# Raw scores stored negated, their column maximum added by an accumulating DMA, running maxima kept pairwise in SBUF, and new instruction orders

## The chip, the cores and the metric

The kernel runs on one core of a Trainium2 chip. The metric is the device time of one execution in microseconds (us). Five instruction queues run side by side and meet at semaphores: TensorE (PE in the profile), VectorE (DVE), ScalarE (ACT), GpSimd (POOL) and SyncE (SP), which here only issues DMAs. Each queue runs its instructions strictly in the order in which the program was written. Matrix products land in PSUM, which TensorE, VectorE and ScalarE reach; GpSimd and DMAs work on SBUF and HBM only.

## The reference

```python
def _A_ref(x, wqkv, wo):                      # S = 2048, D = 448, H = 16, Dh = 28
    qkv = (x @ wqkv).reshape(B, S, 3, H, Dh).transpose(2, 0, 3, 1, 4)
    q, k, v = qkv[0], qkv[1], qkv[2]
    scores = einsum("bhqd,bhkd->bhqk", q, k) * (Dh ** -0.5)
    p = softmax(scores, axis=-1)
    o = einsum("bhqk,bhkd->bhqd", p, v)
    return o.transpose(0, 2, 1, 3).reshape(B, S, D) @ wo
def _B_ref(x, W_gate, W_up, W_down):          # F = 1792
    gate = x @ W_gate; up = x @ W_up
    gate = gate * (gate > 0)
    return (gate * up) @ W_down
g = sigmoid((x * gate_w).sum(-1, keepdims=True))
return g * _A_ref(x, wqkv, wo) + (1 - g) * _B_ref(x, W_gate, W_up, W_down)
```

All tensors are float32. The kernel multiplies with rounded float32 operands and splits each operand into a high part and a low part (the rest), so that several products make up one exact one; `TERMS` lists the eleven products for a depth of 448.

## The kernel before, in words

Three stages follow each other. First the projections: `qk` and `vproj` make queries, keys and values from x, and write queries and keys to HBM. Last comes the feed-forward tail: `down`, `wout` and `result`. Between them, from about 137 us to about 1076 us, lies the attention, 32 visits long, and the first 51 of 56 gate-and-up units of the feed-forward part are laid between its instructions as filling.

A visit is one head (28 channels) and one half of the keys (1024 of 2048). It makes 16 score tiles of 128 keys x 1024 (two chunks of 128 x 512, in PSUM); together they cover all 2048 queries, in four blocks of 512. For query blocks 0 to 2 the softmax maximum is known beforehand: `smax` (line 169) computes the scores a second time with queries on partitions, VectorE reduces them (L171), and `smax_end` writes the negated maximum into spare rows of Q, so that the score product already has it subtracted. ScalarE then takes exp straight out of PSUM (L260). For the last query block (j = 3, four of the sixteen tiles, the "late" ones) the maximum is found from the transposed scores themselves: ScalarE copies the raw scores to SBUF (L262); `block_max` (L228) folds the two chunks of each tile into a running maximum `rm` of 128 x 512 on VectorE, reading PSUM; `all_max` (L234) takes the maximum over partitions on GpSimd; `take_max` (L239) subtracts it on VectorE from each of the two groups of 128 x 2048; `take_exp` (L246) takes exp of a group on ScalarE. `rescale` (L585 to L589) brings the first half's result to the second half's maximum. `pv` (L601) multiplies with the values, in two parts P and Q of 32 matmuls each, the whole 64 taking 7.0 us; P reads the first group, Q the second.

The order is written out by hand as a string for each visit: `FIRST` for visit 0, `LONG` for 24 visits, `WIDE` for 4, and `LATE` for the last 3. A letter is one action: `s` a score tile (two matmuls and the ScalarE instruction that empties it), `m` one `smax` step (two matmuls and one VectorE reduction), `x` one of the eleven matmuls of half a gate-and-up unit, `A` `all_max`, `d` `take_max`, `e` `take_exp`, `n` `smax_end`, `c` and `f` the two parts of `rescale`, `w` the splitting of the next gate-and-up weights (`split_f`), `P` and `Q` the two parts of `pv`. In `FIRST`, `l` sends the last projected keys and `u` splits the second half of the first weights and clears a query buffer. The scores run `AHEAD` = 3 tiles ahead of the visit, so three of a visit's four late tiles are computed near the end of the visit before, and the fourth at its own start.

PSUM holds the score and `smax` tiles in three buffers that are used in turn (`ps_w`), whatever reads them. So a tile's matmuls wait until the tile three before has been read. `split_f` takes the high part of the weights on ScalarE (`act_high`, L103) and the low part, in the attention stage, on GpSimd (`pool_low`, L112).

Of the kernel before, what the change touches and what calls it, by code (L numbers as in the profile page):

```python
# [19 lines left out]
P = 128  # L20
S = 2048
D = 448
H = 16
# [5 lines left out]
NB = 4  # L29
TB = 512  # L30
NK = S // P
SCALE = DH ** -0.5
# [34 lines left out]
def gated_mix_kernel(ctx, tc, x, wq, wo, wgu, wd, out):  # L67
    nc = tc.nc
# [137 lines left out]

    stream = [p for v in range(2 * H) for p in visit(v)]
    todo_max, todo_sub, todo_exp, todo_all = [], [], [], []
    RM = {}

    def block_max(v, j, k, p, q):

        n = TQ[v // 2]
        b = j - NB + n
        if (v, b) not in RM:
            if b == 0:
                rm = att.tile([P, max(TQ), TB], F32, name=f"rm_{v}", tag=f"rm{v % 2}", bufs=1)
                for c in range(n):
                    RM[v, c] = rm[:, c]
        r = RM[v, b]  # L220
        if k % (NK // 2):
            parts = [(p[:, c], r) for c in range(2)]
        elif v % 2:
            parts = [(p[:, 0], RM[v - 1, b]), (p[:, 1], r)]
        else:
            parts = [(p[:, 0], q[:, 1])]
        for x, y in parts:
            nc.vector.tensor_tensor(r, x, y, op=OP.max)  # L228
        if k % (NK // 2) == NK // 2 - 2:
            todo_all.append((v, b, [(v, j, i) for i in (k // 4 - 1, k // 4)]))  # L230

    def all_max():
        v, b, quads = todo_all.pop(0)
# [2 lines left out]

    def take_max():
        v, b, q = todo_sub.pop(0)
        nc.vector.tensor_tensor(QUAD[q], QUAD[q], RM[v, b].unsqueeze(1).to_broadcast([P, 4, TB]), op=OP.subtract)  # L239
        todo_exp.append(q)  # L240

    def take_exp():
        q = min(todo_exp, key=lambda q: (q[0], q[2], q[1]))
        todo_exp.remove(q)
        q = QUAD[q].rearrange("p c t -> p (c t)")
        nc.scalar.activation(q, q, AF.Exp, scale=SCALE)  # L246

    def score(late=True):

        v, done, q, half, chunks = stream.pop(0)  # L250
        h = v // 2
        if q not in QUAD:
            QUAD[q] = p_slot(next(slots) % NP, f"P_{v}_{q[1]}_{q[2]}")
        ps = ps_w(f"s_{v}_{chunks[0][0]}_{chunks[0][1]}")
        for c, (k, j) in enumerate(chunks):
            nc.tensor.matmul(ps[:, c], K[h % 3][:, k * P:(k + 1) * P], Q[h][:, j * TB:(j + 1) * TB], start=True, stop=True)  # L256
            AT[v, k, j] = QUAD[q][:, 2 * half + c]
        dst = QUAD[q][:, 2 * half:2 * half + 2]
        if done:
            nc.scalar.activation(dst, ps, AF.Exp, scale=SCALE)  # L260
        else:
            nc.scalar.activation(dst, ps, AF.Copy)  # L262
# [25 lines left out]
    with tc.tile_pool(name="qkv", bufs=1) as pa:  # L288
# [187 lines left out]
        for n, (f, *a) in enumerate(mixed):  # L476
            if n == 0:
                split_w(*w5)
            if n == 6:
                load_k(1)  # L480
                load_q(1)
            if n == 8:
                split_w(*w3)
            if n == 13:

                nc.gpsimd.memset(f32(K[2])[96:128], -1.0)
            if n == len(mixed) - 6:
# [8 lines left out]
            news = [(score, False) for back in EARLY if back == len(mixed) - n]  # L496
# [22 lines left out]
    def split_f(i, high, low, part=(0, 1)):  # L519

        if part[0] == 0:
            WS[i] = fe.tile([P, 2, 7, P], F32R, name=f"wg_{i}", tag="wg", bufs=2)
        w, wr = WS[i], WR[i]
        for s in part:
            high(w[:, s, 0:3], wr[:, s, 0:3])
            low(w[:, s, 3:6], wr[:, s, 0:3], w[:, s, 0:3])
        if part[-1] == 1:
            high(w[:, :, 6], wr[:, :, 3])
            low(w[64:, :, 6], wr[64:, :, 3], w[64:, :, 6])
            del WR[i]  # L530
            ws_d[i] = dram.tile([P, 2, 7, P], F32, name=f"ws_d_{i}")
            nc.sync.dma_start(ws_d[i], f32(w))
# [58 lines left out]
    PO = {}  # L591
# [63 lines left out]
        if h and q == 2:  # L655
            normalise(h - 1)

    split_f(0, act_high, pool_low, (0,))
    fetch_f(1)
    while todo_max:  # L660
        block_max(*todo_max.pop(0))
    for v, (order, nu) in enumerate(ROUNDS):
        todo = list(range(nxt, nxt + nu))
        nxt += nu
        small_things(2 * v)
        passes = [(*divmod(k, 2), n) for k in todo for n in range(NT)]
        units = []
        ns = 0
        for o in order:
            if o == "x" and not passes:  # L670
                continue
            if o == "s":
                ns += 1
                if ns == 8:
                    small_things(2 * v + 1)
                if stream:
                    score()
            elif o == "m":
                if m < len(maxima):
                    smax(m)  # L680
                    m += 1
            elif o == "x":
                i, half, n = passes.pop(0)
                if n == 0:
                    units.append((i, half, ps_x(f"gu_{i}_{half}")))
                gu_mm(units[-1][2], i, half, n)
                if n == NT - 1:
                    i, half, ps = units.pop()
                    spill_h(i, ps) if half else relu(i, ps)
                    if half:  # L690
                        load_f(i + 2)
            elif o == "n":
                if v % 2 and v < 2 * H - 1:
                    smax_end(v // 2 + 1)
            elif o == "w":
                ready = nxt + (ROUNDS[v + 1][1] if v + 1 < len(ROUNDS) else 2)
                ready = min(ready + ready % 2, 2 * NF)
                while parts < ready:
                    split_f(parts // 2, act_high, pool_low, (parts % 2,))
                    parts += 1  # L700
                    if parts % 2 == 0:
                        fetch_f(parts // 2 + 1)
            elif o == "A":
                all_max()
            elif o == "d":
                take_max()
            elif o == "e":
                take_exp()
            elif o in "cf":
                rescale(v, "cf".index(o))  # L710
            elif o == "l":
                sends.pop()()
            elif o == "u":
                split_f(0, act_high, pool_low, (1,))
                QS.append(last_q("Q2"))
                nc.gpsimd.memset(f32(QS[2])[96:128], 0.0)
# [6 lines left out]
        left = [k for k in todo_exp + todo_sub + todo_all if k[0] == v]  # L723
        assert not passes and not left and v not in PO or len(stream) == max(0, 16 * (2 * H - 1 - v) - AHEAD), (v, passes, left, len(stream) + 16 * (v + 1))
    assert not stream and m == len(maxima), (len(stream), m)
    stk.close()

# [181 lines left out]
```

## Time and profile before

| | |
|---|---|
| median of 3 runs | 1284.88 us (1283.1 to 1288.92) |
| the profiled execution | 1281.88 us, its span 1280.1 us |
| busy, TensorE / VectorE / ScalarE / GpSimd | 1241.6 / 962.1 / 776.1 / 191.2 us |
| span from the first P of visit 0 to the first P of visit 28 | 821.88 us |
| mean share of time that the 16 DMA engines are busy, in that stretch | 0.42 |

A busy TensorE is not TensorE at its peak: matmuls overlap each other, and one row's duration (about 398 ns) is longer than the distance from one to the next. The distance is read from the chain of work that ended last, which lists consecutive matmuls without overlap. The idle time in front of an instruction is named with what released it. In the tables by stretch of time the columns are: length, busy time of TensorE, of its weight loads, of VectorE, ScalarE and GpSimd (with their numbers of instructions), the granted TensorE clock as a share of full speed, the busy share of the DMA engines, and GB/s.

### The profile page before, as it was taken

Reading aid. Unit: us, or ns where it says so; the run is one execution under the profiler, and the core shown is the slowest. Engines: PE = TensorE matmul, PEld = TensorE weight load, DVE = VectorE, ACT = ScalarE, POOL = GpSimd, SP = SyncE. Lnnn points to the kernel's source line nnn. Section 1 sums busy time; section 2 is a strip of 40 time slices with the busy share of each in tenths; the row PEclk is TensorE's granted clock in tenths of the full one; section 3 lists DMA queues with packets and bytes.
Section 4 is the critical chain, followed back from the end, with each engine's and each line's share of the span. In section 5 each row is a group of like instructions: output and inputs, shape, how many; then the busy total and the mean of one; then the engine's idle time right before and its main releaser. Section 6 shows DMA issues by size and latency. Waiting matters only on the chain.

```text
span 1280.1 us, 16867 instructions
## 1 busy us (share of the span) xinstructions
PE 1241.6 (97%) x6431; PEld 872.5 (68%) x6431; DVE 962.1 (75%) x1022; ACT 776.1 (61%) x894; POOL 191.2 (15%) x188
## 2 busy tenths in 40 slices
PE   9999699999999999999999999999999999999998
PEld 6888466665656666666666566666666566799998
DVE  6466679898988989998988889898989543563342
ACT  5223377777877677777777677767777784122121
POOL 4222221221221000000000001000000010551020
PEclk9999899999999999999999999999999999999999
DMA  9845275352626543342536243342442325745432
GB/s 323 289 189 222 84 209 117 127 163 72 169 76 201 169 121 84 103 133 64 163 104 186 81 113 103 84 130 93 132 128 76 119 90 195 228 147 159 132 115 80
DMA packets 64269, 178.37 MB, mean 139 GB/s; under 512 B 13730, under 2 KB 20578, under 8 KB 59554
## 3 DMA queue, kind: packets, MB, share of 16 engines
q1 hardware_dynamic: 57452, 151.00, 39.5%
q0 software_dynamic: 6304, 25.82, 5.3%
q8 instruction: 51, 0.84, 0.3%
q10 hardware_dynamic: 432, 0.46, 0.1%
q14 instruction: 30, 0.25, 0.1%
HBM read 118.58 MB, written 58.87 MB: 139 GB/s over the span
## 4 chain that ended last, share of the span: by engine, by line
PE 89%; DVE 4%; ACT 2%; DMA 2%; issue 1%; POOL 1%; SPq 0%; POOLq 0%; ACTq 0%
PE gu L547 19%; PE s L256 19%; PE po L601 18%; PE sm L169 13%; PE acc L808 10%; PE qk L381 5%; DVE rm L228 3%; PE wo L767 3%; PE v L399 3%; ACT P L262 1%; DVE mx L171 1%; DMA wg<-ws_d 1%; DMA or<-o_d 0%; DMA wr<-wq 0%; ACT P L260 0%
## 5 line engine op out<-in xcount | busy, mean ns | idle before, releaser
L171 DVE TENSOR_REDUCE mx<-sm 128x1 f32<-128x1024 f32 x384 | 456.5, 1219 | 60.6 <-PE sm L169 59.5
L547 PE MATMUL gu<-X,wg 128*128 128x512 f32 x1232 | 373.9, 398 | 10.8 <-POOL wg L112 7.2
L260 ACT ACTIVATE P<-s 128x1024 f32<-128x1024 f32 x306 | 306.7, 1025 | 116.8 <-PE s L256 113.1
L256 PE MATMUL s<-Q,K 128*128 128x512 f32 x1024 | 319.5, 403 | 13.6 <-DVE rm L228 11.2
L547 PEld LDWEIGHTS gu<-X,wg 128*128 128x128 f32 x1232 | 231.6, 189 | 69.1 <-POOL wg L112 7.6
L256 PEld LDWEIGHTS s<-Q,K 128*128 128x128 f32 x1024 | 184.7, 189 | 99.3 <-DVE rm L228 10.9
L169 PE MATMUL sm<-K,Q 128*128 128x512 f32 x768 | 243.2, 398 | 7.5 <-DVE mx L171 3.6
L601 PE MATMUL po<-P,V 128*32 128x512 f32 x1640 | 227.3, 594 | 0.0
L228 DVE TENSOR_TENSOR rm<-s,rm 128x512 f32<-128x512 f32 x218 | 150.4, 690 | 74.6 <-ACT P L262 57.3
L169 PEld LDWEIGHTS sm<-K,Q 128*128 128x128 f32 x768 | 137.1, 188 | 52.6 <-ACT P L260 10.1
L234 POOL PARTITION_ALL_REDUCE rm<-rm x32 | 57.2, 1788 | 673.7 <-DVE rm L228 618.8
L601 PEld LDWEIGHTS po<-P,V 128*32 128x32 f32 x1640 | 62.6, 110 | 116.2 <-issue 111.5
L808 PE MATMUL acc<-WD,hh 128*128 128x448 f32 x672 | 138.5, 365 | 0.0
L262 ACT ACTIVATE P<-s 128x1024 f32<-128x1024 f32 x104 | 105.1, 1024 | 46.6 <-PE s L256 45.4
L808 PEld LDWEIGHTS acc<-WD,hh 128*128 128x128 f32 x672 | 126.2, 188 | 10.4
L239 DVE TENSOR_TENSOR P<-P,rm 128x2048 f32<-128x2048 f32 x52 | 117.9, 2272 | 5.8 <-POOL rm L234 5.8
L601 PE MATMUL po<-V 128*32 128x512 f32 x408 | 115.0, 594 | 0.0
L103 ACT ACTIVATE hh<-hr 128x512 fp32r<-128x512 f32 x56 | 35.2, 631 | 117.8 <-PE acc L808 113.8
L246 ACT ACTIVATE P<-P 128x2048 f32<-128x2048 f32 x52 | 99.4, 1914 | 5.3 <-DVE P L239 4.5
L260 ACT ACTIVATE V<-s 128x1024 f32<-128x1024 f32 x78 | 78.9, 1025 | 37.1 <-PE s L256 35.2
L109 DVE TENSOR_TENSOR hh<-hr,hh 128x512 fp32r<-128x512 f32 x56 | 49.4, 883 | 62.2 <-ACT hh L103 62.2
L381 PE MATMUL qk<-X,W 128*128 128x512 f32 x308 | 77.4, 398 | 0.3 <-DVE X L109 0.2
(79 smaller groups left out, 772.4 us busy)
## 6 DMA issues: line engine op xcount, KB each, us to landing
wg<-ws_d SPq DMA_DIRECT2D x42, 896.0 KB
K<-qk_d SPq DMA_DIRECT2D x64, 224.0 KB
Q<-qk_d SPq DMA_DIRECT2D x64, 224.0 KB
h_d<-h SPq DMA_DIRECT2D x56, 256.0 KB
hr<-h_d SPq DMA_DIRECT2D x56, 256.0 KB
ws_d<-wg SPq DMA_DIRECT2D x14, 896.0 KB
qk_d<-st POOLq DMA_DIRECT2D x21, 512.0 KB, 3.2
wgr<-wgu SPq DMA_DIRECT2D x13, 512.0 KB
```

The source lines that it names most:

```text
L169: nc.tensor.matmul(ps[:, c, :], Q[h][:, u * P:(u + 1) * P], K[h % 3][:, k0:k0 + TB], start=True, stop=True)
L171: nc.vector.tensor_reduce(MX[h][:, 2 * u + half:2 * u + half + 1], ps, axis=AX.XY, op=OP.max)
L228: nc.vector.tensor_tensor(r, x, y, op=OP.max)
L239: nc.vector.tensor_tensor(QUAD[q], QUAD[q], RM[v, b].unsqueeze(1).to_broadcast([P, 4, TB]), op=OP.subtract)
L246: nc.scalar.activation(q, q, AF.Exp, scale=SCALE)
L256: nc.tensor.matmul(ps[:, c], K[h % 3][:, k * P:(k + 1) * P], Q[h][:, j * TB:(j + 1) * TB], start=True, stop=True)
L260: nc.scalar.activation(dst, ps, AF.Exp, scale=SCALE)
L262: nc.scalar.activation(dst, ps, AF.Copy)
L381: nc.tensor.matmul(ps, W[:, a, c * P:(c + 1) * P], xf(tb, b), start=(n == 0), stop=(n == NT - 1))
L547: nc.tensor.matmul(ps, WS[i][:, s, a], xf(i // NF, b), start=(n == 0), stop=(n == NT - 1))
L601: nc.tensor.matmul(po[32 * j:32 * j + 32], V[:, h // 4 % 2, k, h % 4], AT.pop((v, k, j)), start=(k == k0), stop=(k == k0 + NK // 2 - 1))
L808: nc.tensor.matmul(ACC[i // NF][t][:, :D], HH[i][:, a, t * P:(t + 1) * P], WD[:, f, b], start=(f == 0 and n == 0), stop=(f == NF - 1 and n ...
```

## The change

The raw scores of the late tiles are copied out of PSUM with the sign turned (`scale=-1.0`), so the running maximum becomes a running minimum. It is no longer read from PSUM: the new `block_min` (letter `b`, three per visit) folds whole 128 x 1024 tiles in SBUF into a pair `r2`, and the third one folds the pair into `rm` (128 x 512), and turns the sign back. For the second half of the keys the last step also takes the maximum with the first half's `rm`. `take_max` becomes a DMA that GpSimd issues; it adds `rm`, repeated four times, to the group of 128 x 2048 in SBUF (1024 KB each, two per visit, 64 in all). The exp after it uses `scale=-SCALE`. All four late tiles of a visit are now computed in the visit before (`AHEAD` = 4). The low parts of the gate-and-up weights are computed on VectorE (`low`) in place of GpSimd (`pool_low`). The four order strings are new; the numbers of `s`, `m` and `x` in `LONG`, `WIDE` and `LATE` are as before.

```diff
-AHEAD = 3
+AHEAD = 4
-FIRST = "AmxmxsmxmxxlxsxumsmmmxxxsxdxxxsxssmxxmxsmmxdexxsxsewsPQ"
-LONG = "ssmnAxxxxsmxsxmxsmxxxmsmxxxsmxxmxsdxsxxxsxsmxxxsmxxmexxsmxxdxxcsxsefwsPQ"
-WIDE = "smnmxxxxxxxsxxmxxxxmsxmxxsmxxsAmxsxmxxsxsmxdxsxxsssxxxmxxxcsxmsxxdxxmxxxxexsxewsPfQ"
-LATE = "snwsxxAxdxxxsxxsxxxsxxdsxxxxcsxxsxxxsxxxsxxxxsxsxxxxsxxxxxexxxsxxessPfQ"
+FIRST = "xxxbsbbmxmlxssmsxxmuAddsxxsmsxxmxsmsxmsxmxbxsmxmxbxxxesxmebPwQ"
+LONG = "nssAddxxxxmxsxmxxsmxsxmxsxsxmxxsxmsxmxxsmxsxmxssxcxsmxexxmxxxssbxxbbexfmPwQ"
+WIDE = "ssAddnscxxxsxxxmxxxsxxmxsxmxsxmxsxxxmsxxmfxsxxsmsxxxxmxxsxmsxmxxxxmbxexsxxsxbemxxbxPwQ"
+LATE = "nsAddsxxcxsxsxsxxxxxsxxsxssxxxxsxxsxxxssxxwxxexsxxxxxxxbxxxxssxbxxbxexxPfQ"
...
+    def block_min():
...
+        v, j, p = todo_max[0]
+        b = j - NB + TQ[v // 2]
+        if (v, b) not in R2:
+            R2[v, b] = att.tile([P, 2, TB], F32, name=f"r2_{v}_{b}", tag="r2", bufs=1)
+            left[v, b] = NK // 4 - 2
+            nc.vector.tensor_tensor(R2[v, b], todo_max.pop(0)[2], todo_max.pop(0)[2], op=OP.min)
+            return
+        nc.vector.tensor_tensor(R2[v, b], R2[v, b], todo_max.pop(0)[2], op=OP.min)
...
+        nc.vector.tensor_tensor(r, r2[:, 0], r2[:, 1], op=OP.min)
+        if v % 2:
+            nc.vector.scalar_tensor_tensor(r, r, -1.0, RM[v - 1, b], op0=OP.mult, op1=OP.max)
         else:
-            parts = [(p[:, 0], q[:, 1])]
-        for x, y in parts:
-            nc.vector.tensor_tensor(r, x, y, op=OP.max)
...
+            nc.vector.tensor_scalar(r, r, -1.0, None, op0=OP.mult)
...
     def take_max():
         v, b, q = todo_sub.pop(0)
-        nc.vector.tensor_tensor(QUAD[q], QUAD[q], RM[v, b].unsqueeze(1).to_broadcast([P, 4, TB]), op=OP.subtract)
+        nc.gpsimd.dma_start(QUAD[q], RM[v, b].unsqueeze(1).to_broadcast([P, 4, TB]), accum_op=OP.add)
...
-        nc.scalar.activation(q, q, AF.Exp, scale=SCALE)
+        nc.scalar.activation(q, q, AF.Exp, scale=-SCALE)
...
-            nc.scalar.activation(dst, ps, AF.Copy)
-            job = (v, chunks[0][1], chunks[0][0], ps if late else dst, dst)
-            if late:
-                block_max(*job)
-            else:
-                todo_max.append(job)
+            nc.scalar.activation(dst, ps, AF.Copy, scale=-1.0)
+            todo_max.append((v, chunks[0][1], dst))
...
-    split_f(0, act_high, pool_low, (0,))
+    split_f(0, act_high, low, (0,))
     fetch_f(1)
-    while todo_max:
-        block_max(*todo_max.pop(0))
...
-                if ns == 8:
+                if ns == 10:
                     small_things(2 * v + 1)
...
-                    split_f(parts // 2, act_high, pool_low, (parts % 2,))
+                    split_f(parts // 2, act_high, low, (parts % 2,))
...
+            elif o == "b":
+                block_min()
...
-                split_f(0, act_high, pool_low, (1,))
+                split_f(0, act_high, low, (1,))
```

More of the change, by code (lines that the diff above doesn't have):

```diff
@@ L39 @@
 EARLY = (5, 4, 4, 3, 2, 2, 1, 1)
-AHEAD = 3
+AHEAD = 4
 NP = 10
-FIRST = "AmxmxsmxmxxlxsxumsmmmxxxsxdxxxsxssmxxmxsmmxdexxsxsewsPQ"
-LONG = "ssmnAxxxxsmxsxmxsmxxxmsmxxxsmxxmxsdxsxxxsxsmxxxsmxxmexxsmxxdxxcsxsefwsPQ"
-WIDE = "smnmxxxxxxxsxxmxxxxmsxmxxsmxxsAmxsxmxxsxsmxdxsxxsssxxxmxxxcsxmsxxdxxmxxxxexsxewsPfQ"
-LATE = "snwsxxAxdxxxsxxsxxxsxxdsxxxxcsxxsxxxsxxxsxxxxsxsxxxxsxxxxxexxxsxxessPfQ"
+FIRST = "xxxbsbbmxmlxssmsxxmuAddsxxsmsxxmxsmxsmxsmxbxsmxmxbxxxesxmebPwQ"
+LONG = "nssAddxxxxmxsxmxxsmxsxmxsxsxmxxsxmsxmxxsmxsxmxssxcxsmxexxmxxxssbxxbbexfmPwQ"
+WIDE = "ssAddnscxxxsxxxmxxxsxxmxsxmxsxmxsxxxmsxxmfxsxxsmsxxxxmxxsxmsxmxxxxmbxexsxxsxbemxxbxPwQ"
+LATE = "nsAddsxxcxsxsxsxxxxxsxxsxssxxxxsxxsxxxssxxwxxexsxxxxxxxbxxxxssxbxxbxexxPfQ"
 ROUNDS = [(FIRST, 2)] + [(WIDE, 4) if k % 7 == 2 else (LONG, 3) for k in range(2 * H - 4)] + [(LATE, 4)] * 3
@@ L208, in gated_mix_kernel @@
     todo_max, todo_sub, todo_exp, todo_all = [], [], [], []
[L209 to L224, printed above, removed]
-        else:
-            parts = [(p[:, 0], q[:, 1])]
-        for x, y in parts:
-            nc.vector.tensor_tensor(r, x, y, op=OP.max)
-        if k % (NK // 2) == NK // 2 - 2:
-            todo_all.append((v, b, [(v, j, i) for i in (k // 4 - 1, k // 4)]))
+    RM, R2, left = {}, {}, {}
+    def block_min():
+        if not todo_max:
+            return
[5 more added lines that the diff above has]
+            nc.vector.tensor_tensor(R2[v, b], todo_max.pop(0)[2], todo_max.pop(0)[2], op=OP.min)
+            return
+        nc.vector.tensor_tensor(R2[v, b], R2[v, b], todo_max.pop(0)[2], op=OP.min)
+        left[v, b] -= 1
+        if left[v, b]:
+            return
+        r, r2 = att.tile([P, TB], F32, name=f"rm_{v}_{b}", tag=f"rm{v % 2}{b}", bufs=1), R2[v, b]
+        RM[v, b] = r
+        nc.vector.tensor_tensor(r, r2[:, 0], r2[:, 1], op=OP.min)
+        if v % 2:
+            nc.vector.scalar_tensor_tensor(r, r, -1.0, RM[v - 1, b], op0=OP.mult, op1=OP.max)
+        else:
+            nc.vector.tensor_scalar(r, r, -1.0, None, op0=OP.mult)
+        q = NK // 8 * (v % 2)
+        todo_all.append((v, b, [(v, j, q), (v, j, q + 1)]))
     def all_max():
@@ L245, in take_exp, with score @@
         q = QUAD[q].rearrange("p c t -> p (c t)")
-        nc.scalar.activation(q, q, AF.Exp, scale=SCALE)
-    def score(late=True):
+        nc.scalar.activation(q, q, AF.Exp, scale=-SCALE)
+    def score():
         v, done, q, half, chunks = stream.pop(0)
@@ L495, in gated_mix_kernel @@
                 m += 1
-            news = [(score, False) for back in EARLY if back == len(mixed) - n]
+            news = [(score,) for back in EARLY if back == len(mixed) - n]
             for k, c in enumerate(news):
@@ L722, in gated_mix_kernel @@
                 pv(v, "PQ".index(o))
-        left = [k for k in todo_exp + todo_sub + todo_all if k[0] == v]
-        assert not passes and not left and v not in PO or len(stream) == max(0, 16 * (2 * H - 1 - v) - AHEAD), (v, passes, left, len(stream) + 16 * (v + 1))
+        rest = [k for k in todo_exp + todo_sub + todo_all if k[0] == v]
+        assert not passes and not rest and v not in PO or len(stream) == max(0, 16 * (2 * H - 1 - v) - AHEAD), (v, passes, rest, len(stream) + 16 * (v + 1))
     assert not stream and m == len(maxima), (len(stream), m)
```

## The prediction

> **What bounds the kernel now.** I read the page first, then the chain of work that ended last, then busy time by stretch.
>
> ```profile
> span 1280.1 us, 16867 instructions
> PE 1241.6 (97%) x6431; PEld 872.5 (68%) x6431; DVE 962.1 (75%) x1022; ACT 776.1 (61%) x894; POOL 191.2 (15%) x188
> PE 89%; DVE 4%; ACT 2%; DMA 2%; issue 1%; POOL 1%; SPq 0%; POOLq 0%; ACTq 0%
> ```
>
> TensorE carries 89% of the chain, so anything taken off VectorE is worth only the time in which TensorE waits for it. The page's run took 1281.88 us, 3.0 us under the median of 1284.88; the sum below is made against 1281.9. One `LONG` visit on the chain (start, length, what), with the bounds of others:
>
> ```profile
> 170.32 7.24 PE po L601 x64
> ...
> 199.47 7.00 PE po L601 x64
> ...
> 495.06 7.00 PE po L601 x64
> 502.06 0.68 PE s L256 x2
> ...
> 502.76 1.03 ACT P L262
> ...
> 503.82 0.70 DVE rm L228
> ...
> 504.54 0.70 DVE rm L228
> ...
> 505.38 0.70 PE s L256 x2
> 506.08 0.47 PE sm L169 x2
> ...
> 509.15 0.70 PE gu L547 x3
> ...
> 524.05 7.00 PE po L601 x64
> ...
> 992.20 7.00 PE po L601 x64
> 1017.17 7.00 PE po L601 x64
> ```
>
> Unhindered matmuls follow each other every 0.70/3 = 0.2325 us, and the 64 of `po` take 7.0. A `LONG` visit has 33 `x`, 16 `s` and 12 `m`, 33 + 32 + 24 = 89 matmuls: 20.7 + 7.0 = 27.7 us at full pace, against 28.99 from 495.06 to 524.05. Nearly all that is missing lies in one place. After `po`, ScalarE copies the late tile, VectorE folds its two chunks out of PSUM, and only then is the buffer free for the tile three later. From 502.06 to 506.08 there are 12 matmuls (four `s`, two `sm`, four `gu`, two `s` again), 2.79 us of work in 4.02: 1.23 lost, of which 0.68 - 0.465 = 0.22 is the switch from `po`, which stays. So 1.0 us per visit waits for the chain ACT L262, DVE L228, DVE L228.
>
> Over the stage: 170.32 to 992.20 is 821.9 us for 24 `LONG` and 4 `WIDE` visits (11 more matmuls, 30.25 at full pace). 24 x 27.69 + 4 x 30.25 = 785.6; so 36.3 us are lost in all, 1.30 per visit, which agrees. From 992.20 to 1017.17, a `LATE` visit, it is 24.97 against 17.67 + 7.0 = 24.67: nothing to win there.
>
> ```profile
> 495.06:524.05 28.99, 28.19 (x157) 18.21 (x161) 26.03 (x28) 21.04 (x22) 1.83 (x2) 1.00 0.46 116
> 137.00:170.00 33.00, 21.27 (x66) 14.46 (x66) 21.96 (x25) 13.16 (x18) 7.35 (x7) 0.79 0.42 111
> 170.32:992.20 821.88, 804.88 (x4347) 519.42 (x4350) 730.36 (x744) 603.51 (x644) 87.77 (x81) 1.00 0.42 122
> ```
>
> The second row is `FIRST`: TensorE idles 11.7 of 33 us, and the clock granted there is 0.79.
>
> **The change part by part.**
>
> ```profile
> L171 DVE TENSOR_REDUCE mx<-sm 128x1 f32<-128x1024 f32 x384 | 456.5, 1219 | 60.6 <-PE sm L169 59.5
> L228 DVE TENSOR_TENSOR rm<-s,rm 128x512 f32<-128x512 f32 x218 | 150.4, 690 | 74.6 <-ACT P L262 57.3
> L239 DVE TENSOR_TENSOR P<-P,rm 128x2048 f32<-128x2048 f32 x52 | 117.9, 2272 | 5.8 <-POOL rm L234 5.8
> L262 ACT ACTIVATE P<-s 128x1024 f32<-128x1024 f32 x104 | 105.1, 1024 | 46.6 <-PE s L256 45.4
> L246 ACT ACTIVATE P<-P 128x2048 f32<-128x2048 f32 x52 | 99.4, 1914 | 5.3 <-DVE P L239 4.5
> L234 POOL PARTITION_ALL_REDUCE rm<-rm x32 | 57.2, 1788 | 673.7 <-DVE rm L228 618.8
> L109 DVE TENSOR_TENSOR W<-wr,W 128x336 fp32r<-128x336 f32 (+6 forms) x20 | 8.2, 435 | 5.9 <-ACT W L103 5.6
> x_d<-X POOLq DMA_DIRECT2D x6, 1024.0 KB, 5.1
> qk_d<-K POOLq DMA_DIRECT2D x6, 512.0 KB, 6.9
> ```
>
> *VectorE.* Removed per visit: 7.5 folds (7 or 8 by turns) x 0.69 = 5.2 and 2 subtractions x 2.27 = 4.5. Added: 3 minima of 128 x 1024 (half a subtraction 1.14, two folds 1.38; I take 1.2, nearer the subtraction, which is in SBUF too) = 3.6; a last fold 0.7; the sign, between nothing and another fold, 0.4. That is 9.7 against 4.7: 26.0 busy in the quoted visit becomes 21.0. The low parts of the weights: 28 of 128 x 384 at some 0.49 (435 ns for 336 columns, scaled) and 14 smaller ones at 0.36, 19 us in all, 2 us in each of the first ten visits; 23 of 28 there is still room, so I cost it at nothing. What would take that cover away is in the next paragraphs: VectorE standing still.
>
> *The PSUM wait.* The fourth late tile moves into the visit before (`AHEAD` = 4), and PSUM is released by the copy alone. After `po` the first two tiles are plain exps, and `LONG` puts four `x` and a `m` before the third. The 1.0 us goes. What is late next there is the ScalarE copy, 1.0 us after its matmuls, with 1.6 us to go before the buffer is wanted again.
>
> *ScalarE.* The negated copy is the same instruction with another constant: 1.02 us, no cost. But its order matters. Counting 0.2325 per matmul in the new `LONG`, scores stand at 14.4, 14.9, 15.8, then the first `e` at 17.0, scores at 18.6 and 19.1, the second `e` at 20.0, P at 20.7 and Q at 24.2. ScalarE can start the first of those copies at about 15.3; three copies of 1.02 bring it to 18.4, `e` (1.91) to 20.3, two copies to 22.3, the second `e` to 24.2, with a relu (0.6) in some visits 24.8. Q is due at 24.2. So between 0 and 0.6 us come back as a wait before Q; I take 0.2. The gain per visit is then 0.8, over 28 visits 22.4 us.
>
> *The DMA in place of the subtraction.* GpSimd issues two after each `A`; nothing in this trace accumulates by DMA. From below, t is the 5.1 us of a plain 1024 KB transfer issued by GpSimd; from above, twice the 6.9 us that 512 KB took in a busier stretch, 13.8. The accumulation reads two operands where the plain one reads one: I take twice 5.1 = 10.2. Does it fit? The third and fourth late copies end at 21.3 and 22.3; the last minimum, fold and sign bring `rm` to 24.6 in the visit. `A` takes 1.8, the first issue 0.9, and both transfers, one after the other in one queue, 2t; then the second `e` 1.9 and part Q 3.5. This must end by the end of the next visit: 24.6 + 1.8 + 0.9 + 2t + 1.9 + 3.5 = 32.7 + 2t, at most two visits. So the visit is at least 16.35 + t long: no loss up to t = 11.5 (27.9 us visits), back to the old 28.95 at t = 12.6. At 10.2 it is hidden behind matmuls of the next visit. Behind a waiting `e` on ScalarE stand all later score copies, hence TensorE within three tiles. On GpSimd only the small memset of the next `m` tile is queued behind the two issues.
>
> A copy that adds is, by the Trainium skill ("Collectives: The Full Stack", section on the bandwidth ceiling), slow not for the addition but because it reads twice; with the fit of "DMA: Bandwidth & Descriptors" (2.0 us and 436 KB per us, section on the anatomy of a DMA) that is an estimate of 2.0 + 2 x 1049/436 = 6.8 us, and the sum would come out near 1259. The same page says that DMAs of all issuers interleave on the same 16 engines; no run here yet shows either for an accumulation.
>
> *`FIRST`.* Rows of GpSimd's and TensorE's timelines (start, length, in brackets the idle time before):
>
> ```profile
> 144.31 1.80 POOL L234 PARTITION_ALL_REDUCE rm<-rm  x1 [5.62 <-DVE mx L171]
> 147.12 0.90 POOL L388 DMA_DIRECT2D qk_d<-pair  x1 [1.01 <-DVE pair L109]
> 156.04 1.78 POOL L112 TENSOR_TENSOR wg<-pair,wg 128x384 fp32r<-128x384 f32 x2 [8.01 <-issue]
> 157.88 1.80 POOL L716 MEMSET Q<- 32x2048 f32 x1
> 157.87 0.79 PE L547 MATMUL gu<-X,wg 128*128 128x512 f32 x1 [7.18 <-POOL wg L112]
> qk_d<-pair POOLq DMA_DIRECT2D x1, 512.0 KB, 3.3
> L234 POOLq MODIFY_POOL_CONFIG  x18: 1/6/16, 138.7 to 386.7; - x18
> ```
>
> GpSimd's program is switched 18 times here, between `A` and the low parts; the lulls of 5.6 and 8.0 us stand at such switches. With the low parts on VectorE the 7.2 us wait of TensorE goes, and the switching in the attention shrinks to one. But the new order puts that one late: `l` sends `pair` (after low, three `b` and two `m`, 8.3 us of VectorE: 145.5), issue 0.9 and landing 3.3 make 149.7, the memset of the query buffer, which is the same memory as `pair`, must wait for that (151.5), the switch 5.6 to 8.0 (158), `A` 1.8, issue 0.9 (161), t = 10.2, exp 1.9: P starts at 173, against 170.3. With t = 5.1 it would be 168. I count 2.7 us lost.
>
> Other parts (`small_things` at the tenth score, `w` behind P) change the place of short instructions that have 7 us of `po` or most of a visit as cover: nothing, at worst the second `e`'s 0.6 again.
>
> The sum: 1281.9 - 22.4 + 2.7 = 1262.2. I predict 1262, and let the 3 us between this run and the median count as noise; 0.5% (6.4 us) is what a measurement can tell from no change.
>
> **The rivals.**
>
> *The transfers are late (slower).* The loop above decides, from t = 12.6 on. For it speaks that the engines are already busy 0.42 of this stage, and that 6.9 us for 512 KB was seen; against it the plain 5.1. At t = 13.8 a visit takes 30.15: 1.2 x 28 = 33.6 more, and `FIRST` 6 more: 1322. Worse: twice 5.1 with only 0.58 of the engines free is 17.6, the visit 33.95, 140 us more. By the two pages' figures it would be 6.8/0.58 = 11.7, just beyond the free range.
>
> *ScalarE takes the stall over (no change).* If the second exp ends 0.9 later than Q is due, the gain is eaten: 1281.9 - 28 x 0.1 + 2.7 = 1282. For it: three scores within 1.9 us before the first `e`; against: ScalarE is busy only 21.0 of 29.
>
> *All of it goes.* No wait at Q, the whole 36.3 us, and VectorE alone bounding `FIRST` (25 us of work before P, 8 us saved): 1281.9 - 36 - 8 = 1238.
>
> **How the numbers follow.** Forecast with its gains between these two ends 0.62, of which 0.06 for the last rival; late transfers 0.26; stall moved 0.12. The likeliest case alone gives 1245 to 1273 (all of the 1.0 us and t = 5.1, or 0.6 back in each visit with t = 12). Both signs are possible: 1240 to 1318 leaves out the 1238 end and the severe half of the late transfers, about 0.18. The moved stall falls within 0.5% mostly, a little of it to the faster side: faster 0.64, same 0.09, slower 0.27.
>
> **What would show it.** Right: the chain from the end of `po` runs through `s` and `gu` without the L262 and L228 pieces; visits near 28.1 us; VectorE near 21 us per visit; accumulations landing in 7 to 12 us; ScalarE without waits on a DMA. Wrong: ScalarE's exp in place waiting for the DMA with TensorE idle behind it, visits above 29 us; P of visit 0 far from 173; or `gu` waiting for its weights' DMA, which share the engines.

## The result, and the profile after

The changed kernel takes 1376.97 us (median of 4 runs, 1368.23 to 1381.7) against 1285.73: 1.070 times as long, 95% interval 1.064 to 1.076. The forecast was 1262, with 1240 to 1318 as its range; it was wrong in sign.

The page of the changed kernel, whose profiled execution has a span 99.8 us longer than before (1379.9 against 1280.1):

```profile
span 1379.9 us, 16858 instructions
PE 1266.4 (92%) x6431; PEld 884.1 (64%) x6431; DVE 850.4 (62%) x920; ACT 773.0 (56%) x894; POOL 240.0 (17%) x210
q1 hardware_dynamic: 57452, 151.00, 36.8%
q0 software_dynamic: 40096, 92.94, 33.4%
PE 64%; DMA 22%; issue 4%; DVE 4%; SPq 3%; POOL 1%; ACT 1%; POOLq 0%; DVEq 0%; ACTq 0%
```

VectorE was relieved as meant: 850 us busy in place of 962. But DMAs, 2% of the chain before, are 22% of it now. The queue in which GpSimd's DMAs run (q0) takes 33.4% of the 16 engines' span, 461 us, against 5.3%, 68 us, before: 393 us for 64 accumulations, 6.1 us each of all sixteen engines.

The time was lost between the first P of visit 0 and that of visit 28. Two stretches by time, from the first P of visit 1 to that of visit 28 (27 visits), of the kernel before and then of the changed one; the columns are as in the tables shown earlier:

```profile
199.40:992.13 792.73, 776.18 (x4190) 500.52 (x4189) 704.54 (x719) 580.66 (x616) 80.54 (x74) 1.00 0.42 120
```

```profile
213.25:1089.51 876.26, 797.69 (x4189) 511.83 (x4189) 608.77 (x628) 578.44 (x616) 124.14 (x95) 0.96 0.77 174
```

83.5 us more in these visits, and 13.9 us more before them. The DMA engines' busy share went from 0.42 to 0.77, and the granted clock to 0.96. The 83.5 us divide into 62.0 in which TensorE stands (it idles 876.26 - 797.69 = 78.6 us in place of 16.6) and 21.5 by which its busy time grew for the same matmuls, beside the lowered clock. What TensorE waited for in these 27 visits of the changed kernel (in total, times, longest):

```profile
PE s L260 <- DVE mx L171: 48.0, 15, 8.4
PE gu L547 <- DMA X<-x_d: 12.8, 3, 10.6
...
PE gu L547 <- DMA wg<-ws_d: 2.6, 2, 2.0
PE po L601 <- ACT P L250: 2.4, 1, 2.4
PE po L601 <- ACT V L250: 1.7, 1, 1.7
```

Most of it waits for VectorE's `smax` reductions, and only 4.1 us for exp. A visit is no longer even: eight of the 27 take 36 to 43 us, the others 27.9 (1 us less than a long visit before) to 34.0. In two of the eight the wait is another: the gate-and-up matmuls stand 10.6 us for the reload of x in one (41.0 us), and 8.5 us in the other (41.2 us), 2.1 of them for x and 6.3 for nothing that the profile names. The chain in two of them (start, length, what), the first slow, the second quick:

```profile
280.38 7.00 PE po L601 x64
...
289.89 17.43 DMA ls<-os
...
307.34 0.07 DVE rq L616
...
308.73 2.07 PE s L260 x4
...
317.98 7.00 PE po L601 x64
...
963.91 7.03 PE po L601 x64
...
991.85 7.05 PE po L601 x64
```

In the slow one the chain runs through an 8 KB transfer that has nothing to do with the score maxima: the row sums of the head before (`ls`), of which VectorE takes the reciprocal at L616. VectorE's own timeline in another slow visit, and the list of who waited for whom (in total, times, longest):

```profile
365.26 2.38 DVE L171 TENSOR_REDUCE mx<-sm 128x1 f32<-128x1024 f32 x2 [0.40 <-PE sm L169]
376.44 0.25 DVE L616 RECIPROCAL rq<-ls 128x16 f32<-128x16 f32 x1 [8.81 <-DMA ls<-os]
376.61 2.29 DVE L171 TENSOR_REDUCE mx<-sm 128x1 f32<-128x1024 f32 x2
```

```profile
PE s L260 <- DVE mx L171: 48.3, 16, 8.4
...
DVE os L627 <- DMA rb<-l_d: 57.6, 10, 13.8
DVE rq L616 <- DMA ls<-os: 44.6, 13, 11.3
...
ACT P L250 <- DMA P<-rm: 30.7, 11, 14.4
```

VectorE stands 102 us in all at two short instructions that before the change never waited for a DMA. Behind them in its queue stand the `smax` reductions, and behind those TensorE's next score tiles. A stretch of 32 us around the wait of 8.81 us shows what goes with it: the DMA engines are 0.93 busy, and TensorE's clock is 0.84.

```profile
352.00:384.00 32.00, 23.48 (x103) 16.43 (x96) 18.21 (x22) 16.80 (x19) 3.69 (x4) 0.84 0.93 215
```

The accumulations themselves, median and extremes from issue to landing:

```profile
P<-rm POOLq DMA_DIRECT2D x52, 1024.0 KB, 13.8
DMA to landing us min/median/max: 8.0/13.8/31.5
```

From visit 1 on to visit 27, in the second visit of a head the first of a pair lands after 8.2 to 15.0 us and the second after 13.6 to 22.4; in the first visit, where SP's queue loads 1.8 MB of keys and queries (eight transfers of 224 KB), after 8.4 to 19.2 and 21.7 to 31.5.

### The profile page after: what moved, and what is told of

The parts are those of the page before. It is cut to its first block, busy times and chain, and to the rows that moved or that the text cites. A ratio compares the mean times of both kernels' runs of the same rounds, so it can differ in the third digit from the quotient of the medians.

```text
span 1379.9 us, 16858 instructions
## 1 busy us (share of the span) xinstructions
PE 1266.4 (92%) x6431; PEld 884.1 (64%) x6431; DVE 850.4 (62%) x920; ACT 773.0 (56%) x894; POOL 240.0 (17%) x210
## 3 DMA queue, kind: packets, MB, share of 16 engines
q0 software_dynamic: 40096, 92.94, 33.4%
## 4 chain that ended last, share of the span: by engine, by line
PE 64%; DMA 22%; issue 4%; DVE 4%; SPq 3%; POOL 1%; ACT 1%; POOLq 0%; DVEq 0%; ACTq 0%
PE gu L547 13%; PE po L601 13%; PE s L260 12%; PE acc L808 9%; PE sm L169 8%; DMA ls<-os 6%; DMA K<-qk_d 5%; PE qk L381 5%; DMA l_d<-rq 3%; PE wo L767 2%; PE v L399 2%; DMA P<-rm 2%; DMA rb<-l_d 2%; DVE mx L171 2%; DMA wg<-ws_d 1%
## 5 line engine op out<-in xcount | busy, mean ns | idle before, releaser
L171 DVE TENSOR_REDUCE mx<-sm 128x1 f32<-128x1024 f32 x384 | 464.0, 1221 | 183.7 <-PE sm L169 182.8
L547 PE MATMUL gu<-X,wg 128*128 128x512 f32 x1232 | 399.9, 406 | 27.7 <-DMA X<-x_d 12.8
L264 ACT ACTIVATE P<-s 128x1024 f32<-128x1024 f32 x306 | 306.0, 1024 | 207.1 <-PE s L260 199.7
L260 PE MATMUL s<-Q,K 128*128 128x512 f32 x1024 | 323.0, 411 | 55.2 <-DVE mx L171 48.3
L547 PEld LDWEIGHTS gu<-X,wg 128*128 128x128 f32 x1232 | 238.4, 194 | 88.9 <-DMA X<-x_d 14.7
L169 PE MATMUL sm<-K,Q 128*128 128x512 f32 x768 | 247.8, 404 | 6.9 <-ACT P L264 4.2
L601 PE MATMUL po<-P,V 128*32 128x512 f32 x1640 | 234.0, 601 | 14.9 <-ACT P L250 14.9
L169 PEld LDWEIGHTS sm<-K,Q 128*128 128x128 f32 x768 | 141.3, 194 | 51.9 <-ACT P L264 16.6
L266 ACT ACTIVATE P<-s 128x1024 f32<-128x1024 f32 x104 | 102.2, 1029 | 17.3 <-PE s L260 16.6
L264 ACT ACTIVATE V<-s 128x1024 f32<-128x1024 f32 x78 | 78.6, 1026 | 34.4 <-PE s L260 31.4
L222 DVE TENSOR_TENSOR r<-r,P 128x1024 f32<-128x1024 f32 x52 | 63.7, 1225 | 17.7 <-ACT P L266 13.4
L243 POOL DMA_DIRECT2D P<-rm x52 | 72.1, 1595 | 9.5 <-POOL rm L238 9.5
## 6 DMA issues: line engine op xcount, KB each, us to landing
P<-rm POOLq DMA_DIRECT2D x52, 1024.0 KB, 13.8
```

The costliest lines, as they stand in the source:

```text
L169: nc.tensor.matmul(ps[:, c, :], Q[h][:, u * P:(u + 1) * P], K[h % 3][:, k0:k0 + TB], start=True, stop=True)
L171: nc.vector.tensor_reduce(MX[h][:, 2 * u + half:2 * u + half + 1], ps, axis=AX.XY, op=OP.max)
L222: nc.vector.tensor_tensor(R2[v, b], R2[v, b], todo_max.pop(0)[2], op=OP.min)
L243: nc.gpsimd.dma_start(QUAD[q], RM[v, b].unsqueeze(1).to_broadcast([P, 4, TB]), accum_op=OP.add)
L266: nc.scalar.activation(dst, ps, AF.Copy, scale=-1.0)
L547: nc.tensor.matmul(ps, WS[i][:, s, a], xf(i // NF, b), start=(n == 0), stop=(n == NT - 1))
```

## The experiments

Three theories were put against each other. E: the accumulations keep the engines busy, SP's small transfers land late, and VectorE waits for them in order. L: the loop of the forecast's rival, exp in place waits for its own accumulation. O: the new orders lose by themselves. A ratio is to the kernel before, with its 95% interval.

### The addition on VectorE

```diff
-        nc.gpsimd.dma_start(QUAD[q], RM[v, b]...to_broadcast([P, 4, TB]), accum_op=OP.add)
+        nc.vector.tensor_tensor(QUAD[q], QUAD[q], RM[v, b]...to_broadcast([P, 4, TB]), op=OP.add)
```

> The changed kernel with one part undone: the repeated maximum is added on VectorE (two instructions of 128 x 2048 per visit, at the same places in the orders) and no accumulating DMA is left. Theory E (the accumulations keep the 16 DMA engines busy, the small transfers of SP's queue land late, and VectorE, in order, stands at the reciprocal L616 and the multiplication L627): the 45 and 58 us of waits there go to nearly nothing, time 1262 to 1295. Theory L (my forecast's rival: exp on ScalarE waits for its own accumulation): the same fall, since the transfer is gone. Theory O (the new orders lose by themselves, whatever does the addition): still above 1350.

Measured: 1350.35 us, ratio 1.051 (1.048 to 1.054). The waits at L616 and L627 for DMAs are gone, as E says, but the time fell by only 27 us: visits now take 30.1 to 34.9 us for another reason. VectorE has the two additions (4.6 us) again, in a burst at the start of the visit, ahead of the `smax` reductions, and TensorE waits 68.7 us for L171. So with the addition back on VectorE these orders lose too. E and L had put the time at 1262 to 1295, and O, above 1350, comes in by a third of a us only. All three theories were too simple here.

### Plain copies in place of accumulations

```diff
-        nc.gpsimd.dma_start(QUAD[q], RM[v, b]..., accum_op=OP.add)
+        nc.gpsimd.dma_start(QUAD[q], RM[v, b]...)
```

> The changed kernel with the 64 DMAs as plain copies of the same source and shape: the raw scores of the last query block are overwritten instead of added to, so those outputs are not the reference's. One read per write in place of two. Theory E: engine time per transfer falls from 6 us to about 3, waits at L616 and L627 fall to about half, time 1300 to 1340. Theory L: landing falls from 13.8 below 10 us, exp waits no more, time 1262 to 1290. Theory O: unchanged, above 1360. If it is not the bytes but the 2 KB pieces, landing stays near 13 us and time near 1370.

Measured: 1286.09 us, ratio 1.000 (0.998 to 1.002): 91 us less than the changed kernel for this one word. Two lines of its DMA view, and the same stretch of 27 visits:

```profile
q0 software_dynamic: 23712, 92.94, 19.1%
P<-rm POOLq DMA_DIRECT2D x52, 1024.0 KB, 7.7
```

```profile
203.46:995.01 791.55, 774.09 (x4189) 500.26 (x4188) 612.04 (x628) 576.19 (x616) 93.65 (x95) 0.99 0.61 192
```

19.1% of 1285.1 us less the 68 is 178 us, 2.8 us of engine time per transfer in place of 6.1. The bytes counted in q0 are the same; the clock is back at 0.99, L616 waits 12.8 us in place of 44.6 and L627 3.6 in place of 57.6. In the second half of the stage almost every long visit takes 27.9 us. O is out: with these orders and with the same 64 DMAs of the same size, it is the adding that costs. Between E and L this run does not decide, since a plain copy is both cheaper for the engines (2.8 us, where E expected about 3) and earlier to land (7.7 us in the median, where L expected below 10). The time lies in L's range and below E's (1300 to 1340), and the waits at L616 and L627 fell further than the half that E expected. In the slow kernel itself the list of TensorE's waits decides for E: 48.0 us for the reductions behind VectorE's waits against 4.1 for exp.

### The reciprocal and the multiplication late

```diff
-        if h and q == 1:
+        if h and q == 2:
             row_sums(h - 1)
             spread(h - 1)
-        if h and q == 2:
-            normalise(h - 1)
+        if h > 1 and q == 0:
+            normalise(h - 2)
...
-            RS[h] = fe.tile([P, TB], F32, name=f"rs_{h}", tag="rb", bufs=1)
+            RS[h] = RM[v - 1, 0]
...
-LONG = "...xmxxxssbxxbbexfmPwQ"
+LONG = "...xmxxxssfbxxbbexmPwQ"
-LATE = "...xxwxxexsxxxxxxxbxxxxssxbxxbxexxPfQ"
+LATE = "...xxwxxexsfxxxxxxxbxxxxssxbxxbxexxPQ"
```

> The changed kernel, accumulations kept, with the reciprocal of a head's row sums half a head later and its multiplication a whole visit after that (and the rescaling difference kept in place, its second part a little earlier, to make room), so that VectorE reaches them long after their transfers. Theory E: waits at L616 and L627 go (102 us together), time falls by 50 to 90 us, to 1287 to 1327. Theory L: exp waits for the accumulation as before, time within 10 us of 1377. Theory O: within 10 us of 1377.

Measured: 1402.0 us, ratio 1.092 (1.090 to 1.094), slower than the changed kernel by some 25 us, where E had promised 50 to 90 us less. VectorE no longer waits for `ls` or `rb` at all. In their place (list of waits, then the chain over one visit):

```profile
ACT P L250 <- DMA P<-rm: 79.1, 16, 14.3
```

```profile
PE po L601 <- ACT P L250: 64.6, 14, 12.5
```

```profile
511.72 25.76 DMA P<-rm
537.50 1.92 ACT P L250
539.47 3.62 PE po L601 x26
```

Exp now waits for its accumulation, 25.8 us from issue to landing, and TensorE for exp: the loop of theory L, though the time lies outside L's range too (within 10 us of 1377). So the waits at L616 and L627 had been hiding that loop, and to take them away uncovered it: TensorE idles 79.5 us between the first P of visit 1 and that of visit 28, as much as in the changed kernel (78.6), but 65.8 of them now for exp. The two are two faces of one shortage, and E in the narrow form (that the time comes back when VectorE's waits are taken away) fell. The edit also moves the second part of the rescaling (`f`) forward; the next run shows that with plain copies these moves cost nothing.

### The same with plain copies

```diff
 (the kernel above, and)
-        nc.gpsimd.dma_start(QUAD[q], RM[v, b]..., accum_op=OP.add)
+        nc.gpsimd.dma_start(QUAD[q], RM[v, b]...)
```

> The version with the late reciprocal and multiplication, its DMAs as plain copies (the raw scores of the last query block are overwritten, so those outputs are not the reference's). If that version was slow because exp then waited for accumulations that landed after 15 to 30 us (the loop of my forecast's rival), plain copies, which land after 5 to 15 us, leave no wait at all: 1255 to 1285, below the plain copies without the late reciprocal. If moving the reciprocal and the rescaling harmed by itself, it stays above 1300.

Measured: 1281.31 us, ratio 0.996 (0.995 to 0.998). The late reciprocal harms nothing where the DMA engines have room; it gains 5 us over plain copies alone. The chain of a visit of the plain-copy kernel without it, for comparison with the quick visit above:

```profile
539.63 7.00 PE po L601 x64
546.84 0.93 PE s L260 x4
...
567.52 7.00 PE po L601 x64
```

27.89 us, with no piece of ScalarE or VectorE in it.

### Traffic alone, in the kernel before

```diff
+    dump = [dram.tile([P, 4, TB], F32, name=f"dump_{r}") for r in range(2)]
...
     def all_max():
...
+        for r in range(2):
+            nc.gpsimd.dma_start(dump[r], f32(X[0][r]))
```

> The kernel before, unchanged in what it computes, with two plain 1024 KB copies per visit added (SBUF to a scratch tensor in HBM, issued by GpSimd after each partition maximum; nothing waits for them). Theory E: traffic alone delays SP's small transfers; waits at L616 and L627 appear (10 to 50 us), time 1290 to 1330; at half the engine time of an accumulation, perhaps only a part of the loss. Theory L: nothing waits for these copies, time within 8 us of 1285. Theory O: within 8 us of 1285.

Measured: 1294.93 us, ratio 1.007 (1.005 to 1.010), 10 us more. Nearly all of it lies in one visit, which goes from 29.3 to 39.3 us, and its chain runs from an added copy (8.0 us) to the reload of x (5.1 us), which overwrites the tile that I had chosen as the copies' source and so must wait for them. That is a flaw of the experiment and not a delay by traffic. In the other visits nothing is lost: L616 does not wait for a DMA, L627 1.9 us in all. So two plain transfers per visit, some 2.6 us of engine time each, do no harm in the orders of before, against what E expected. But the run does not show that only the dearer accumulations can do harm, because the place of the big transfers differs too. The issue of the big transfers and of `ls` (start, length), first in the changed kernel, then in this run:

```profile
625.74 2.64 POOL L243 DMA_DIRECT2D P<-rm  x2 [0.30 <-POOL rm L238]
627.26 0.63 SPq L611 DMA_DIRECT2D ls<-os  x1
```

```profile
603.82 1.08 POOL L238 DMA_DIRECT2D dump<-X  x2
628.53 0.64 SPq L614 DMA_DIRECT2D ls<-os  x1
```

In the changed kernel `ls` of every head but the last leaves 0.6 to 5.6 us behind the second accumulation, and its last packet ends 9.9 to 16.7 us after its issue; in this run it leaves 18 us or more behind the copies, which have landed by then, and from the fifth head on it is through 1.6 us after its issue, as in the kernel before. With plain copies in the new orders, close ahead of `ls` as the accumulations are, it takes 5.5 to 11.0 us. So the place, right behind the burst, and the adding both delay the small transfer; no run here changes the place alone.

### A flat source

```diff
-        nc.gpsimd.dma_start(QUAD[q], RM[v, b]..., accum_op=OP.add)
+        nc.gpsimd.dma_start(QUAD[q], f32(X[0][0]), accum_op=OP.add)
```

> The changed kernel with the source of the accumulations exchanged for a flat tile of the same size (a part of x, 8 KB in a row per partition, in place of 2 KB repeated four times), so the maximum is not added and the outputs of the last query block are not the reference's. If the doubled engine time comes from reading two operands, nothing changes: 8 us for the first and 16 for the second at best, about 6 us of engine time each, time 1360 to 1390. If it comes from the 2 KB pieces of the repeated source, landing falls towards that of plain copies (5 and 10 us) and the time to 1280 to 1310.

Measured: 1391.11 us, ratio 1.080 (1.075 to 1.084).

```profile
q0 software_dynamic: 15520, 92.94, 29.2%
P<-X POOLq DMA_DIRECT2D x52, 1024.0 KB, 12.7
```

The packets of q0 fall from 40096 to 15520, the engine time only to 29.2% of 1391.7 less 68, 338 us or 5.3 us each, and landing from 13.8 to 12.7. The time does not fall with them (1391 against 1377 us). So the piece size is a small part; with either size of pieces an accumulation costs about twice a plain transfer (6.1 against 2.8, and 5.3 against the 2.6 of the copies to HBM above).

### Half the dose, twice

```diff
-        nc.gpsimd.dma_start(QUAD[q], RM[v, b]..., accum_op=OP.add)
+        if q[2] % 2:
+            nc.vector.tensor_tensor(QUAD[q], QUAD[q], RM[v, b]..., op=OP.add)
+        else:
+            nc.gpsimd.dma_start(QUAD[q], RM[v, b]..., accum_op=OP.add)
...
-LONG = "nssAddxxxxm...smxsxmxssxcxsmx..."
+LONG = "nssAdxxxxm...smxsdxmxssxcxsmx..."
```

> Half the dose: of the two groups of a visit the first is still added by an accumulating DMA right after the partition maximum, the second on VectorE at about 13 us. If the engine time of the accumulations is the cause (about 6 us of all 16 engines each), the busy share in the visits falls from 0.77 to about 0.6, the one transfer lands after 8 to 12 us, waits at L616 and L627 shrink below 20 us together and exp does not wait: time 1265 to 1300. If any accumulation in the visit suffices to delay the small transfers, it stays above 1340.

Measured: 1326.31 us, ratio 1.030 (1.028 to 1.033). The busy share is 0.60, and L616 and L627 wait 12 us together, as expected, but the time lies above the expected 1265 to 1300: all but one of the long visits of the second half take 29.2 to 29.8 us, now with TensorE waiting for VectorE. So the other way round, with the orders of the changed kernel as they are:

```diff
-        nc.gpsimd.dma_start(QUAD[q], RM[v, b]..., accum_op=OP.add)
+        if q[2] % 2 == 0:
+            nc.vector.tensor_tensor(QUAD[q], QUAD[q], RM[v, b]..., op=OP.add)
+        else:
+            nc.gpsimd.dma_start(QUAD[q], RM[v, b]..., accum_op=OP.add)
```

> Half the dose the other way round: the first group of a visit is added on VectorE at the visit's start, where VectorE has just had the 7 us of the value product without work, and the second, whose exp is due some 3 us later, by an accumulating DMA. The busy share of the engines should be that of the other half dose, 0.6; if VectorE's place is what held that version at 29.3 us per visit, visits now take 28.0 to 28.8 and the time is 1265 to 1300. If one accumulation per visit still delays the small transfers enough, waits at L616 and L627 stay above 20 us and the time above 1305.

Measured: 1293.65 us, ratio 1.005 (1.003 to 1.007), 83 us less than the changed kernel with one of two additions taken off the DMA engines. A stretch of 800 us of it:

```profile
206.00:1006.00 800.00, 784.50 (x4267) 500.54 (x4269) 677.38 (x667) 582.97 (x621) 90.43 (x70) 1.00 0.62 155
```

All but one of the long visits of the second half take 27.9 to 28.8 us, less than before the change; what is left is lost early: P of visit 1 at 210.3 against 199.4 (VectorE waits 13.4 us for the first partition maximum), and visits of 29.5 to 31.9 while weights are split on VectorE. With the late reciprocal added to it:

> The same with the reciprocal and the multiplication moved late as in the earlier version. With one accumulation per visit landing after 8 to 12 us, neither VectorE nor exp should wait for a DMA: 1258 to 1285, the fastest of all if the two causes are the only ones. If it comes out no faster than its neighbour without the move, those waits were not what was left.

Measured: 1318.34 us, ratio 1.025 (1.023 to 1.028), 25 us slower than its neighbour. No DMA holds VectorE at L616 or L627 and exp waits for none, so those waits were not what was left; TensorE waits 37.6 us for L171 in place of 24.6. Why the move costs 25 us where VectorE also carries one addition, and nothing where it carries none, was not followed further.

### The additions on VectorE, moved apart

```diff
 (as the first experiment, and)
-LONG = "nssAddxxxxmxsxmxxsmxsxmxsxsxmxxsxmsxmxxsmxsxmxssxcxsmx..."
+LONG = "nssAxxxxmxsxmxxsmxsxmxsxsxmdxxsxmsxmxxsmxsxmxssdxcxsmx..."
```

> The changed kernel with the addition on VectorE and its two instructions moved apart, to about 8 and 15 us into a visit, where the subtractions of the kernel before stood. It tells whether the 30 us visits of the version with both additions at the visit's start come from that place. If so, visits return to about 28 to 29 us and the time to 1262 to 1295. If the minima out of SBUF or the new orders cost by themselves, it stays above 1330.

Measured: 1335.19 us, ratio 1.038 (1.036 to 1.040); visits of 29.6 to 34.8 us. The place is worth 15 us, not 60. The other branch of the expectation holds: without the DMA the rest of the change loses some 50 us. One group of VectorE's rows shows why:

```profile
L243 DVE TENSOR_TENSOR P<-P,rm 128x2048 f32<-128x2048 f32 x52 | 118.5, 2283 | 11.8 <-POOL rm L238 11.8
L222 DVE TENSOR_TENSOR r<-r,P 128x1024 f32<-128x1024 f32 x52 | 63.7, 1224 | 5.2 <-DVE r L220 0.5 <-ACT P L266 0.3
L228 DVE TENSOR_TENSOR rm<-r 128x512 f32<-128x512 f32 x32 | 22.2, 692 | 1.1
```

The minima in SBUF save almost nothing: per visit 3 x 1.22 + 0.69 + 0.43 or 0.69 = 4.9 us where 7.5 folds of 0.69 were 5.2; with the weights' low parts (20 us in all) VectorE has no less to do than before (989 us busy in this run, 962 before the change), in orders made for less. The low parts of all later weights back on GpSimd:

```diff
 (the kernel above, and)
-                    split_f(parts // 2, act_high, low, (parts % 2,))
+                    split_f(parts // 2, act_high, pool_low, (parts % 2,))
```

> As the version with the additions on VectorE and moved apart, but the low parts of all later weights on GpSimd, as before the change (the first weights stay on VectorE). About 2 us less on VectorE in each of the first ten visits. If VectorE is full there (25.5 + 2 of 28 us), it is 5 to 20 us faster than that version; if not, within 4 us of it. Against the kernel before: 1255 to 1285.

Measured: 1348.08 us, ratio 1.048 (1.046 to 1.050): 13 us slower, not faster. Visits 3 and 4 take 41.5 and 33.2 us in place of 34.8 and 30.2; the additions and the rescaling now wait 22 us for the partition maximum in place of 12. That it comes late behind GpSimd's work on the weights is likely, but not shown by a run of its own.

### The PSUM wait alone

```diff
-LONG = "ssmnAxxxxsmxsxmxsmxxxmsmxxxsmxxmxsdxsxxxsxsmxxxsmxxmexxsmxxdxxcsxsefwsPQ"
+LONG = "ssmnAxxxxxxxsmxsxmxsmxxmsmxxsmxxmxsdxsxxxsxsmxxsmxxmexxsmxxdxxcsxsefwsPQ"
```

> The kernel before with one edit in the order of the 24 long visits: three gate-and-up matmuls moved from later in the visit to just ahead of the third score tile, in front of which TensorE waits 0.7 to 0.8 us for the copy and two folds of a late tile. If that wait is all there is to it, up to 0.7 us x 24 = 17 us come off: 1268 to 1280. If VectorE (26.0 us busy in a visit of 28.9) is close enough to full that the wait only moves to another tile, the time stays within 5 us of 1285.

Measured: 1296.58 us, ratio 1.008 (1.007 to 1.010). The wait is gone from its place and comes back larger elsewhere. Pieces of the chain of one visit of this kernel:

```profile
509.54 1.64 PE gu L547 x7
...
511.26 0.70 PE s L256 x2
...
513.87 1.24 DVE mx L171 x2
...
520.93 2.89 ACT P L260 x3
...
530.87 7.00 PE po L601 x64
```

All but one of the long visits of the second half take 28.8 to 29.9 us. In the kernel before, VectorE had 26 us of work in 28.9, and moving matmuls alone did not take the wait away here; whether another order could is open.

## Why the prediction was wrong

Right: the wait between the copy, the folds and the score tile is gone, and a long visit without other trouble takes 27.9 us (forecast 28.1); with plain copies nearly every late visit does. VectorE falls to 608.8/27 = 22.5 us per visit, of which 0.7 is weights (forecast 21.0 and the weights). The accumulation's 8.0 us from issue to landing at the earliest lies inside the bounds of 5.1 and 13.8, and 6.1 us of engine time is 2.2 times the 2.8 of a plain copy. The Trainium skill ("Collectives: The Full Stack", section on the bandwidth ceiling) says of the reduce-scatter that it is slow not for the addition but for its two source reads; this factor agrees with it, and so does the flat source, which takes only 0.8 us off the engine time, though no run here counts the reads. The 6.8 us that the prediction estimated from the Trainium skill ("DMA: Bandwidth & Descriptors", section on the anatomy of a DMA) lies below every landing measured, 8.0 to 31.5 us.

Near by luck: `FIRST`. P of visit 0 started at 162 but stood after six matmuls, for 12.6 us, until exp had its accumulation, at 175.6 (forecast 173). Two errors nearly cancel there: `A` started at 163.0, where the working had 158, and the first accumulation landed after 8.0 us, where it had 10.2. And the 2.7 us that the sum counted for this part were 13.9 by the first P of visit 1: TensorE idled those 12.6 us for exp and 5.3 more for the negated maxima, at a clock of 0.83.

Wrong, first, and decisive: the step that costed "other parts (`small_things` ...)" at nothing, covered by "7 us of `po` or most of a visit". What these instructions need is not cover on VectorE but their own transfers in time, on engines to which the change added 12.3 us of work per visit; I priced the new DMAs by their latency alone, and their occupancy only as a multiplier of that latency. The order strings put the pair of accumulations right ahead of `ls`, and its packets, through 1.6 us after its issue from the fifth head on before the change, took 9.9 to 16.7 us in every head but the last. The keys, x and the weights were on the same engines. So 102 us of standing came to VectorE, which works strictly in order, and 48.0 of it reached TensorE.

Wrong, second: t was taken as one number for all visits. 8 us each in a quiet visit would have been free by the bound 16.35 + t. At the start of a head, beside 1.8 MB of SP's loads, the pair takes 21.7 to 31.5 us; with half of that, 10.9 to 15.8, for t, the bound gives 27.2 to 32.1. Where VectorE's waits were taken away, exp did wait for its accumulation, in a mean visit of 32.6 us; but single visits took 27.8 to 46.5, which one number for t cannot give. So the rival of late transfers, priced at 1322, named the right shortage, but its path, through exp, carried only 4.1 us of TensorE's idle time in the changed kernel; its price lacked the small transfers and the lowered clock (0.96 in the stage).

Not wrong, but easily misread: the saving on VectorE, 9.7 against 4.7. Three minima of 1.2 were sized rightly, but 4.5 of the 5.0 hangs on the subtractions leaving VectorE. Without the DMA the rest of the change, in these orders, loses: 1335 and 1350 us.

Two ends of the likeliest case do not follow from its terms: the whole 1.0 us and t = 5.1 give 1281.9 - 28 - 2.3 = 1252, not 1245, and 0.6 back in each visit with t = 12 gives 1275, not 1273. Nothing else hangs on them.

Open: what each wait is worth by itself, since another takes its place when it is removed; what the accumulations would cost if they were issued behind `ls`; and why the late reciprocal costs 25 us with half the dose.

## What to carry to other kernels

A DMA added to a loop has two prices: its latency against the slack of its own consumer, and its engine time against the slack of every other transfer in flight. Before moving work from a busy engine to DMA, add the engine time to the busy share of the stretch where it will run, and look for small transfers that an in-order compute engine will wait for, those issued right behind the new one above all; an accumulation counted double here. And when a wait is removed and the time rises, look for the wait that it was hiding.

## What the runs showed of the hardware

An accumulating DMA of 1024 KB from SBUF to SBUF takes 6.1 us of all sixteen engines (6.0 in the two runs with half of them), 5.3 with 8 KB pieces, against 2.8 for a plain copy between the same tiles; the first of a pair lands after 8.0 us at the earliest (plain 4.6). An issue on GpSimd lasts 1.6 us in the median, where a plain copy between the same tiles took 0.76, and I had taken 0.9. SP pays too: its issue of a key load takes 1.34 us in the median in place of 0.38:

```profile
L148 SPq DMA_DIRECT2D K<-qk_d x64: 307/1335/2268, 36.2 to 1004.6; - x64
```
